# Attention and two mixture-of-experts layers on one core: a front that loads k and v first, gate words a slice earlier, and own buffers for the last sums

## The chip, the cores and the metric

The kernel runs on one core of one Trainium2 chip. The metric is the device time of one execution in microseconds (us); less is better. The engines are TensorE (PE), VectorE (DVE), ScalarE (ACT), GpSimd (POOL) and SyncE (SP), which issues most of the DMAs. Each works through its own queue in order.

## The reference, cut to what matters

`q`, `k` and `v` have 4 batches, 8 heads, 576 tokens and 64 columns a head, all float32. The attention has a softmax of q over the columns and of k over the tokens; then come two layers with 8 experts each.

```
q_s = exp(q - max(q, -1)); q_s /= sum(q_s, -1) + 1e-9
k_s = exp(k - max(k, tokens)); k_s /= sum(k_s, tokens) + 1e-9
kv = einsum('bhsd,bhse->bhde', k_s, v)
x = einsum('bhsd,bhde->bhse', q_s, kv) -> (2304, 512)
expert_idx = argmax(x @ w_gate); gate_w = softmax at expert_idx
x = gate_w * (relu(x @ w1[e]) @ w2[e])     # kept tokens only, capacity 576 an expert
out = x + gate_w2 * (relu(x @ w1b[e]) @ w2b[e])   # where x @ w_skip > 0, else x
```

The second layer has a gate and weights of its own. With these inputs nearly all tokens of a batch go to one expert.

## The kernel before, in words

One batch of 576 tokens is one **group** of a layer: tokens are in the free dimension (two halves of 288), the 512 columns in four chunks of 128 partitions. A group has 16 **slices**: eight of 128 hidden columns for w1 and eight half slices for w2. A slice of w1 is 24 matmuls (two halves, four chunks, three products of high and low parts: `xh`, `xl` of x, `wh`, `wl` of the weights). Split into high and low (`split`, L773): ACT casts (L774), DVE subtracts (L775). ACT evacuates a w1 slice with relu (`hh`, L868), DVE takes the rest (`hl`, L869); both are operands of the w2 slices (L855). Two PSUM tiles, `pair`, alternate between slices.

The order of the work is written out by hand. `COURSE` (L44) has five groups, (layer, batch): (0,0), (0,1), (0,2), (1,0), (1,1). For each of the 16 slices it has a line of words, before the bar and behind it; the loop at the end emits `products(i)`, the split of the weights for slice i+2, the words before the bar, `evacuate(i)`, and the words behind it. A word such as `e.km` is a step of half a batch of attention (a, b: first batch; c, d: second; e, f: third; g, i: fourth, of which no full group is made): `qm` maxima of q, `q1` to `q3` exponentials, `qn` normalisation, `km`, `kt`, `kc`, `ke` the maxima of k, their transposition, subtraction and exponential, `kv` the product k v, `qt` transposes of q, `re` the product with kv. `C1.6` is step 6 of the routing of batch 1. `G.1` and `G.2` make the group's gate a row on all partitions: `gate1` (L903) computes the gate words `gm` on DVE (`gate_weights`, L893: hi, gm, gm), transposes them on PE (pgm, L907), and sends them through DRAM; `gate2` reads them back. Since PE's queue is in order, the next slice stands behind that transposition.

Before the first group stands the **front** (L938 to L1045), written as straight code for the halves a and b of batch 0. Loads are issued on SP in the order q, k of a, k, q of b, then v of both; `warm_up(n)` (L529) issues n matmuls on constants that nobody reads. When one token's x is ready (token 512), `guess` (L560) makes its logits (pgu, L565) and names the expert whose weights SP loads for the group, ahead of the routing; steps 5 and 6 of the routing compare the guess with the list of experts found (L724), and a miss counts into `beyond`. If that is positive at the end, a general branch computes all again. C1.g and C2.g make the same guess for batches 1 and 2. `first_products` (L804) then does the first two slices of group (0,0) in one piece; the course goes on behind them with `C0.1` (pl, L586) and c's maxima of k.

At the end, `evacuate` of a last group multiplies with the gate into `yt` and adds it to x (L886 to L888). `yt` has the tag "ot", a ring of three buffers that the output tiles of `Store` have too; an output tile is free when its DMA has landed.

Of the kernel before, what the change touches and what calls it, by code (L numbers as in the profile page):

```python
# [45 lines left out]
    L4 c.qm | C0.1  # L46
    c.km c.q1 | c.kt
# [18 lines left out]
    L5 C1.6 e.q2 | e.kc  # L66
# [17 lines left out]
    L5 S.p M0.3 | S.g0 M0.4  # L84
# [15 lines left out]
    L4 | g.rw  # L100
# [17 lines left out]
    L4 | T.t03 O0.2  # L118
# [20 lines left out]
def kernel(  # L139
# [410 lines left out]
    class Route:  # L550
# [9 lines left out]
        def guess(self):  # L560

            g = GUESS.index(self.s[1])
            pt = bank("pgu")
            for c in range(NC):
                nc.tensor.matmul(  # L565
                    out=pt[0:1, 0:E], lhsT=self.chunk(c, slice(4 * P, 4 * P + 1)), rhs=self.weights[:, c, 0:E],
                    start=(c == 0), stop=(c == NC - 1),
                )
# [208 lines left out]
    class Group:  # L777
# [26 lines left out]
        def first_products(self):  # L804

            pts = [banks() for _ in range(2)]
            for cs in (range(0, 2), range(2, 4)):
                for s in range(2):
                    wh, wl = whs[s % NB], wls[s % NB]
                    for a in range(2):  # L810
                        for c in cs:
                            for n, (u, w) in enumerate(((wh, xh), (wh, xl), (wl, xh))):
                                nc.tensor.matmul(  # L813
                                    out=pts[s][:, a, :HT],
                                    lhsT=u[:, c],
                                    rhs=w[:, c, tokens(a)],
                                    start=(c == 0 and n == 0),
                                    stop=(c == NC - 1 and n == 2),
                                )
            return pts  # L820

        early = ()
# [40 lines left out]
        def evacuate(self, s):  # L863
# [22 lines left out]
            t = halves(hp.tile([P, S], F32, name="yt", tag="ot", bufs=3))[:, w]  # L886
# [16 lines left out]
        def gate1(self):  # L903

            self.gate_weights()
# [33 lines left out]
    with tc.tile_pool(name="fp", bufs=1) as fp:  # L939
        warm16 = fp.tile([P, 3 * P], F16, name="warm16")  # L940
        nc.vector.memset(warm16, 1.0)
        warm_up(34)
        a, b = [Half(0, hh, X[0], fp, 1) for hh in range(2)]
        a.load_q()
        a.load_k()
        b.load_k()
        b.load_q()
        a.load_v()
        b.load_v()
        H["c"].load_q()  # L950
        H["c"].load_k()
        a.room()
        b.room()
        j4 = [(h, 4) for h in range(HH)]
        a.qm()
        a.exps(j4 + [i for i in HJ if i not in j4])
# [4 lines left out]
        a.kc()  # L961
        warm_up(5)
        b.kt_()
        a.ke()
        warm_up(7)
        b.kc_max()
        a.inverse()
        a.norm(j=slice(4, 5))
        b.kc_sub()
        warm_up(2)  # L970
        a.kv1()
        b.ke()
        b.qm()
        a.norm(slice(0, 2), F4)
        pt = bank("ptq")
        a.turn_new()
        a.turn(0, pt)
        a.kv2()
        nc.scalar.copy(a.qT[:, 0, 0:4 * P], pt)
        b.exps(j4)  # L980
        b.exp_sub(slice(0, 2), F4)
        b.kv1()
        b.exps([(2, j) for j in range(4)])
        b.exp_act(slice(0, 2), F4)
        b.inverse(j=slice(4, 5))
        b.norm(j=slice(4, 5))
        a.norm(slice(2, 4), F4)
        p4 = bank("ptq4")
        b.turn_new()
        a.turn_last(p4)  # L990
        b.turn_last(p4, 2 * LAST)
        a.to_last(nc.scalar.copy, a.qT, p4)
        b.to_last(nc.scalar.copy, b.qT, p4, 2 * LAST)
        b.exps([(3, j) for j in range(4)])
        pt = bank("ptq")
        a.turn(1, pt)
        nc.scalar.copy(a.qT[:, 1, 0:4 * P], pt)
        px = bank("px4")
        a.out_last(px)
        b.sum_bulk(slice(0, 2), F4)  # L1000
        b.kv2()
        b.out_last(px, 2 * LAST)
# [8 lines left out]
        first.load(0, 0)  # L1011
        first.load(0, 1)
        first.load(1)
        H["c"].load_v()
        first.load(2)
        H["d"].load_q()
        H["d"].load_k()
# [397 lines left out]
```

## Time and profile before

| what | before |
|---|---|
| median of 3 runs (lowest to highest) | 442.55 us (441.36 to 442.78) |
| the profiled execution, its span | 443.49 us, 441.7 us |
| PE busy, share of the span | 403.4 us, 91% |
| DVE busy, ACT busy | 250.1 us (57%), 185.8 us (42%) |
| mean granted TensorE clock | 0.948 of full speed |

All times below are from the start of the span. Busy time of PE is modelled and its ends overlap; what a slice takes is better read from the chain of waits or from starts that follow each other. In a table of stretches PEclk is the granted clock as a share of full speed (2.4 GHz); 0.50 is the lower level (1.2 GHz). A name behind an arrow in brackets is what ended an idle time.

### The profile page before, as it was taken

Reading aid. Unit: us, or ns where it says so; the run is one execution under the profiler, and the core shown is the slowest. Engines: PE = TensorE matmul, PEld = TensorE weight load, DVE = VectorE, ACT = ScalarE, POOL = GpSimd, SP = SyncE. Lnnn points to the kernel's source line nnn. Section 1 sums busy time; section 2 is a strip of 40 time slices with the busy share of each in tenths; the row PEclk is TensorE's granted clock in tenths of the full one; section 3 lists DMA queues with packets and bytes.
Section 4 is the critical chain, followed back from the end, with each engine's and each line's share of the span. In section 5 each row is a group of like instructions: output and inputs, shape, how many; then the busy total and the mean of one; then the engine's idle time right before and its main releaser. Section 6 shows DMA issues by size and latency. Waiting matters only on the chain.

```text
span 441.7 us, 8583 instructions
## 1 busy us (share of the span) xinstructions
PE 403.4 (91%) x3297; PEld 359.2 (81%) x3297; DVE 250.1 (57%) x636; ACT 185.8 (42%) x570; POOL 8.3 (2%) x34
## 2 busy tenths in 40 slices
PE   8896799999996999999999999888999999899891
PEld 4673698988996989898999888778998988699881
DVE  3955259743686556357636655366576735554431
ACT  4646357563347474324246522322375333231211
POOL 3000000000000000000000000000000000000000
PEclk9958879999998899999999999998999999999996
DMA  8809812600770400095255671116135555273133
GB/s 210 245 1 258 196 47 88 170 1 1 247 201 0 124 1 1 2 310 137 60 206 174 200 221 47 49 49 217 49 96 170 169 171 177 74 213 132 35 101 84
DMA packets 72537, 54.50 MB, mean 123 GB/s; under 512 B 18455, under 2 KB 67115, under 8 KB 72491
## 3 DMA queue, kind: packets, MB, share of 16 engines
q1 hardware_dynamic: 70536, 53.60, 41.6%
q10 hardware_dynamic: 1954, 0.31, 0.5%
q8 instruction: 27, 0.44, 0.4%
q14 instruction: 20, 0.16, 0.1%
HBM read 49.16 MB, written 4.73 MB: 122 GB/s over the span
## 4 chain that ended last, share of the span: by engine, by line
PE 76%; DVE 10%; ACT 7%; issue 3%; DMA 2%; SPq 0%; DVEq 0%; ACTq 0%
PE pair L855 28%; PE pair L834 24%; PE pk L437 4%; PE pair L813 2%; PE px L495 2%; PE ptq L463 2%; PE pl L586 2%; PE pxs L1084 2%; ACT eq L334 2%; ACT hh L868 1%; PE pto L1218 1%; DMA kt<-in_k_dram 1%; PE py L1140 1%; PE ph L1140 1%; DVE wl L775 1%
## 5 line engine op out<-in xcount | busy, mean ns | idle before, releaser
L855 PE MATMUL pair<-hh,wh 128*128 128x288 f32 x320 | 98.0, 306 | 0.0
L834 PE MATMUL pair<-xh,wh 128*128 128x288 f32 x304 | 96.1, 316 | 0.0
L855 PE MATMUL pair<-hl,wh 128*128 128x288 f32 x320 | 94.4, 295 | 0.0
L855 PE MATMUL pair<-hh,wl 128*128 128x288 f32 x320 | 94.2, 294 | 0.0
L834 PE MATMUL pair<-xl,wh 128*128 128x288 f32 x304 | 92.3, 304 | 0.0
L834 PE MATMUL pair<-xh,wl 128*128 128x288 f32 x304 | 92.1, 303 | 0.0
L775 DVE TENSOR_TENSOR wl<-ws,wh 128x512 fp32r<-128x512 f32 x80 | 54.9, 686 | 38.1 <-ACT wh L774 37.1
L868 ACT ACTIVATE hh<-pair 128x576 fp32r<-128x576 f32 x40 | 25.9, 648 | 108.9 <-PE pair L834 100.1
L869 DVE SCALAR_TENSOR_TENSOR hl<-pair,hh 128x576 fp32r<-128x576 f32 x40 | 30.3, 756 | 62.9 <-ACT hh L868 62.9
L855 PEld LDWEIGHTS pair<-hh,wh 128*128 128x128 f32 x320 | 60.2, 188 | 3.8 <-issue 1.6
L834 PEld LDWEIGHTS pair<-xh,wh 128*128 128x128 f32 x304 | 60.0, 197 | 2.2 <-issue 0.9
L855 PEld LDWEIGHTS pair<-hl,wh 128*128 128x128 f32 x320 | 60.2, 188 | 0.1
L834 PEld LDWEIGHTS pair<-xl,wh 128*128 128x128 f32 x304 | 60.1, 198 | 0.1
L855 PEld LDWEIGHTS pair<-hh,wl 128*128 128x128 f32 x320 | 60.1, 188 | 0.0
L834 PEld LDWEIGHTS pair<-xh,wl 128*128 128x128 f32 x304 | 59.8, 197 | 0.0
L334 ACT ACTIVATE eq<-qt,mx 128x64 f32<-128x64 f32 x152 | 50.7, 337 | 4.7 <-DVE mx L323 4.7
L774 ACT CAST wh<-ws 128x512 fp32r<-128x512 f32 x80 | 49.1, 619 | 2.7 <-DMA ws<-in_moe_w_dram 2.1
L334 ACT ACTIVATION_READ_ACCUMULATOR eq<-qt,mx 128x1 f32 x152 | 28.8, 189 | 0.0
L775 DVE TENSOR_TENSOR xl<-x,xh 128x576 fp32r<-128x576 f32 x20 | 15.0, 753 | 9.0 <-ACT xh L774 9.0
L1219 ACT COPY ot<-pto 128x256 f32<-128x256 f32 (+1 forms) x24 | 7.0, 316 | 28.3 <-PE pto L1218 21.2
L411 ACT ACTIVATE kt<-kt 128x1280 f32<-128x1280 f32 x8 | 10.2, 1272 | 13.8 <-issue 7.1
L437 PE MATMUL pk<-vt,kt 128*64 128x64 f32 (+3 forms) x320 | 15.9, 242 | 0.0
(196 smaller groups left out, 499.8 us busy)
## 6 DMA issues: line engine op xcount, KB each, us to landing
ws<-in_moe_w_dram SPq DMA_DIRECT2D x39, 512.0 KB, 4.9
tw<-in_moe_w_dram SPq DMA_DIRECT2D x24, 512.0 KB, 4.4
qt<-in_q_dram SPq DMA_DIRECT2D x8, 512.0 KB, 7.8
kt<-in_k_dram SPq DMA_DIRECT2D x8, 512.0 KB, 7.5
out_dram<-ot SPq DMA_DIRECT2D x12, 256.0 KB, 2.7
vt<-in_v_dram SPq DMA_DIRECT2D x4, 512.0 KB, 7.0
vt<-in_v_dram SPq DMA_DIRECT2D x16, 128.0 KB, 5.4
mg<-gate SPq DMA_DIRECT2D x4, 288.0 KB, 6.0
```

The lines of the kernel that those rows point to most:

```text
L334: nc.scalar.activation(self.eqv[:, h, j], self.qt[:, h, j], AF.Exp, bias=self.mx[:, i:i + 1], accum_out=self.qz[:, i:i + 1])
L411: nc.scalar.activation(self.kt, self.kt, AF.Exp)
L437: nc.tensor.matmul(out=pk[64 * g:64 * g + 64, c * D1 + o:c * D1 + o + n], lhsT=self.kt[:rows(j), 2 * c + g, j], rhs=ones32[:rows(j), 0:1] ...
L463: nc.tensor.transpose(pt[:, j * P:(j + 1) * P], self.eqf[:, j, c * P:(c + 1) * P], ident)
L495: nc.tensor.matmul(out=pt, lhsT=self.kd[:, c], rhs=self.qT[:, c, 0:4 * P], start=True, stop=True)
L586: nc.tensor.matmul(out=pl[32 * c:32 * c + 32, :HT], lhsT=self.weights[:, c], rhs=self.chunk(c, tokens(a)), start=True, stop=True,)
L774: nc.scalar.copy(hi, src)
L775: nc.vector.tensor_tensor(out=lo, in0=src, in1=hi.bitcast(F32), op=ALU.subtract)
L834: nc.tensor.matmul(out=self.pt[:, a, :HT], lhsT=u[:, c], rhs=w[:, c, tokens(a)], start=(c == 0 and n == 0), stop=(c == NC - 1 and n == 2),)
L855: nc.tensor.matmul(out=self.pt[:, a, :HT], lhsT=p_[:, f], rhs=w[:, tokens(a)], start=(v == 0 and f == 0 and n == 0), stop=(v == 1 and f == ...
L868: nc.scalar.activation(halves(hh), src, AF.Relu)
L869: nc.vector.scalar_tensor_tensor(out=halves(hl), in0=src, scalar=0.0, in1=halves(hh).bitcast(F32), op0=ALU.max, op1=ALU.subtract,)
```

## The change

1. The front. SP loads k of a, k of b, v of a, q of a, v of b, q of b; c's k is loaded only after the first group's first weights. The k path of both halves stands first, with kv for both; then the guess; then q of a and of b, in halves of two heads (five blocks of 64 columns each, one half as DVE addition and one ACT exponential, the other as ten small exponentials, where before token block 4 had its own pass). `warm_up` has 24 instead of 34 at the start and other counts between the steps. `set_capacity` (one matmul and two DVE copies) moves from the front's end to behind b's transposes of maxima.
2. The guess has another input: the sums of the rows of kv (four matmuls of kv with a column of ones, pgx, and a DVE copy gx). All three guesses are made so.
3. The first two slices are done in four parts: the first two chunks of either slice, then the last two. The splits of x and of the weights stand between.
4. `gate_weights` is a word of its own, G.3, one to four slices ahead of G.1.
5. In the last group `yt` takes buffers of another tag ("kqv", seven).
6. In the first line of group (0,0) c.km stands behind `C0.1` and not a slice later.

```diff
     ((0, 0), """
-    L4 c.qm | C0.1
-    c.km c.q1 | c.kt
+    L4 c.qm | C0.1 c.km
+    c.q1 | c.kt
...
-    L5 C1.6 e.q2 | e.kc
+    L5 C1.6 e.q2 | G.3 e.kc
...
-    L5 S.p M0.3 | S.g0 M0.4
+    L5 G.3 S.p M0.3 | S.g0 M0.4
...
-    L4 | g.rw
+    L4 G.3 | g.rw
...
-    L4 | T.t03 O0.2
+    L4 G.3 | T.t03 O0.2
...
             g = GUESS.index(self.s[1])
+            pt = bank("pgx")
+            for c in range(NC):
+                nc.tensor.matmul(
+                    out=pt[:, c:c + 1], lhsT=kvd[c // 2][:, c % 2], rhs=ones32[:, 0:1], start=True, stop=True
+                )
+            gx = self.tl([P, NC], "gx")
+            nc.vector.tensor_copy(out=gx, in_=pt[:, 0:NC])
             pt = bank("pgu")
             for c in range(NC):
                 nc.tensor.matmul(
-                    out=pt[0:1, 0:E], lhsT=self.chunk(c, slice(4 * P, 4 * P + 1)), rhs=self.weights[:, c, 0:E],
+                    out=pt[0:1, 0:E], lhsT=gx[:, c:c + 1], rhs=self.weights[:, c, 0:E],
...
-            t = halves(hp.tile([P, S], F32, name="yt", tag="ot", bufs=3))[:, w]
+            if self.last:
+                t = ap.tile([P, S], F32, name="yt", tag="kqv", bufs=7)
+            else:
+                t = hp.tile([P, S], F32, name="yt", tag="ot", bufs=3)
+            t = halves(t)[:, w]
...
         def gate1(self):
 
-            self.gate_weights()
...
+        def first_products(self, s, cs):
+
+            if cs[0] == 0:
+                self.early = self.early + [banks()]
+            wh, wl = whs[s % NB], wls[s % NB]
+            for a in range(2):
+                for c in cs:
+                    for n, (u, w) in enumerate(((wh, xh), (wh, xl), (wl, xh))):
...
-        warm_up(34)
+        warm_up(24)
         a, b = [Half(0, hh, X[0], fp, 1) for hh in range(2)]
-        a.load_q()
         a.load_k()
         b.load_k()
+        a.load_v()
+        a.load_q()
+        b.load_v()
         b.load_q()
-        a.load_v()
-        b.load_v()
         H["c"].load_q()
-        H["c"].load_k()
...
+        a.km()
+        a.kt_()
+        warm_up(4)
+        b.km()
+        a.kc_max()
+        warm_up(5)
+        a.kc_sub()
+        a.ke()
+        b.kt_()
+        warm_up(5)
+        set_capacity()
+        b.kc_max()
+        warm_up(3)
+        b.kc_sub()
+        a.kv1()
+        b.ke()
+        a.qm()
+        a.exps([(2, j) for j in range(NJ)])
+        a.exp_sub(H01, slice(0, NJ))
+        a.exp_act(H01, slice(0, NJ))
+        warm_up(4)
+        b.kv1()
+        a.exps([(3, j) for j in range(NJ)])
+        a.kv2()
+        b.kv2()
+        warm_up(3)
+        a.sum_bulk(H01, slice(0, NJ))
         RT["C0"].guess()
         first.eid = load_reg(gid[0], [ET.SP], 7)
         first.load(0, 0)
         first.load(0, 1)
         first.load(1)
+        H["c"].load_k()
+        first.load(2)
         H["c"].load_v()
-        first.load(2)
         H["d"].load_q()
         H["d"].load_k()
         first.load(3)
         H["d"].load_v()
...
+        q_norm(a, H01)
+        b.qm()
+        b.exp_sub(H01, slice(0, NJ))
+        a.turn_new()
+        warm_up(3)
+        q_turn(a, 0)
+        b.exps([(2, j) for j in range(NJ)])
+        q_norm(a, H23)
+        b.exp_act(H01, slice(0, NJ))
+        warm_up(3)
+        q_turn(a, 1)
+        q_last(a)
+        x_main(a, 0)
+        b.sum_bulk(H01, slice(0, NJ))
+        b.exps([(3, j) for j in range(NJ)])
+        x_main(a, 1)
+        x_last(a)
+        q_norm(b, H01)
+        first.split_x(0)
+        first.split_x(1)
+        first.split_w(0)
+        q_norm(b, H23)
+        b.turn_new()
+        q_turn(b, 0)
+        first.first_products(0, range(0, 2))
+        q_turn(b, 1)
+        q_last(b)
+        x_main(b, 0)
+        first.split_w(1)
+        x_last(b)
+        x_main(b, 1)
+        first.first_products(1, range(0, 2))
+        first.split_x(2)
+        first.split_x(3)
+        first.first_products(0, range(2, 4))
+        first.first_products(1, range(2, 4))
```

**Three places in the order of instructions.** The first is DVE in group (0,1), from the end of routing step 6 (gw) to the copy of the transposed gate words (gT); kt is e's subtraction of maxima, mx f's maxima of q. Before:

```order
L747 RECIPROCAL gw_136<-gw_136 128x5
L869 SCALAR_TENSOR_TENSOR hl<-pair_84,hh 128x576
L404 TENSOR_TENSOR kt<-kt,pmax 128x1280
L775 TENSOR_TENSOR wl_207<-ws_200,wh_203 128x512
L320 TENSOR_REDUCE mx<-qt 128x20
L323 TENSOR_SCALAR mx<-mx 128x20
L869 SCALAR_TENSOR_TENSOR hl<-pair_83,hh 128x576
L897 TENSOR_SCALAR hi<-dlo_137 128x1
L898 SCALAR_TENSOR_TENSOR gm<-z_135,dlo_137,gw_136 128x5
L901 SCALAR_TENSOR_TENSOR gm<-z_135,hi,gm 128x5
L909 COPY gT<-pgm 5x128
```

and now:

```order
L754 RECIPROCAL gw_136<-gw_136 128x5
L874 SCALAR_TENSOR_TENSOR hl<-pair_83,hh 128x576
L906 TENSOR_SCALAR hi<-dlo_137 128x1
L907 SCALAR_TENSOR_TENSOR gm<-z_135,dlo_137,gw_136 128x5
L910 SCALAR_TENSOR_TENSOR gm<-z_135,hi,gm 128x5
L404 TENSOR_TENSOR kt<-kt,pmax 128x1280
L782 TENSOR_TENSOR wl_207<-ws_200,wh_203 128x512
L320 TENSOR_REDUCE mx<-qt 128x20
L323 TENSOR_SCALAR mx<-mx 128x20
L874 SCALAR_TENSOR_TENSOR hl<-pair_84,hh 128x576
L917 COPY gT<-pgm 5x128
```

The three instructions that make gm moved up past kt, a weight split, both mx and one hl. (Behind the change the lines of the code are other ones: L897 is L906 now.)

The second is DVE in the front, from kv of half b to the guess (gid) and beyond. Before:

```order
L458 TENSOR_TENSOR kvd_115<-pk,rz 64x2x64 x2
L362 TENSOR_SCALAR qz<-qz 128x2x4
L363 RECIPROCAL qz<-qz 128x2x4
L1004 COPY x_121<-px_489 128x4x64
L367 TENSOR_TENSOR eq<-eq,qz 128x2x4x64
L571 TENSOR_REDUCE gmx<-pgu 1x1
L572 SCALAR_TENSOR_TENSOR gsc<-pgu,gmx,c_85 1x8
L575 TENSOR_REDUCE gkey_107<-gsc 1x1
L576 TENSOR_SCALAR gid_110<-gkey_107 1x1
L577 TENSOR_SCALAR gid_110<-gid_110 1x1
```

and now:

```order
L458 TENSOR_TENSOR kvd_115<-pk,rz 64x2x64 x2
L348 TENSOR_REDUCE qz<-eq 128x10
L569 COPY gx<-pgx 128x4
L578 TENSOR_REDUCE gmx<-pgu 1x1
L579 SCALAR_TENSOR_TENSOR gsc<-pgu,gmx,c_85 1x8
L582 TENSOR_REDUCE gkey_107<-gsc 1x1
L583 TENSOR_SCALAR gid_110<-gkey_107 1x1
L584 TENSOR_SCALAR gid_110<-gid_110 1x1
L362 TENSOR_SCALAR qz<-qz 128x10
L363 RECIPROCAL qz<-qz 128x10
L367 TENSOR_TENSOR eq<-eq,qz 128x2x5x64
L320 TENSOR_REDUCE mx<-qt 128x20
```

The copy of x (L1004) that fed the guess is gone; the copy gx of the sums and q's row sums (qz) stand ahead of it, and b's maxima of q (mx) and its subtraction follow the guess instead of preceding kv.

The third is DVE at the program's end, with the semaphores that an instruction waits for (DMAHW are those of the DMA queues); ot is an output tile. Before:

```order
L1219 COPY ot<-pto 128x256 [waits DMAHW1_49,DMAHW2_49,PE_49,Activation_49]
L1219 COPY ot<-pto 128x256 [waits DVE_49,PE_49]
L1219 COPY ot<-pto 128x256 [waits DMAHW3_49,DMAHW4_49,PE_49,Activation_49]
L887 TENSOR_TENSOR yt<-pair_83,mg 128x288 [waits DMAHW0_49,DMAHW7_49,DVE_49,Activation_49]
L888 TENSOR_TENSOR x_122<-x_122,yt 128x288 [waits DVE_49]
L1219 COPY ot<-pto 128x256 [waits DMAHW6_49,DMAHW5_49,PE_49]
```

and now:

```order
L1234 COPY ot<-pto 128x256 [waits DMAHW7_49,DMAHW0_49,PE_49]
L1234 COPY ot<-pto 128x256 [waits DMAHW1_49,DMAHW2_49,PE_49,Activation_49]
L1234 COPY ot<-pto 128x256 [waits DMAHW3_49,DMAHW4_49,PE_49,Activation_49]
L896 TENSOR_TENSOR yt<-pair_84,mg 128x288
L897 TENSOR_TENSOR x_122<-x_122,yt 128x288 [waits DVE_49]
L1234 COPY ot<-pto 128x256 [waits DMAHW5_49,DMAHW6_49,PE_49,Activation_49]
```

The order is the same; the last yt no longer waits for a DMA semaphore.

## Rows read from the trace of the kernel before

**Rows 1.** The page, busy time: us, share of the span, instructions.

```profile
PE 403.4 (91%) x3297; PEld 359.2 (81%) x3297; DVE 250.1 (57%) x636; ACT 185.8 (42%) x570; POOL 8.3 (2%) x34
```

**Rows 2.** What PE waited for, whole span: us in total, times, longest.

```profile
PE pgm L907 <- DVE gm L901: 7.9, 4, 4.1
PE pt L386 <- DVE m L380: 4.5, 3, 3.4
...
PE pto L1218 <- DVE x L888: 3.0, 1, 3.0
```

**Rows 3.** Stretches, PE: length, busy (instructions), clock, DMA share, GB/s.

```profile
20.49:34.14 13.65, 13.65 (x117) 0.50 0.06 18
...
137.10:141.19 4.09, 0.00 (x0) 0.85 0.00 0
141.19:147.07 5.88, 5.88 (x25) 0.52 0.55 137
294.98:296.97 1.99, 0.00 (x1) 1.00 0.00 0
296.97:300.38 3.41, 3.41 (x15) 0.50 0.24 72
```

**Rows 4.** Chain that ended last, 130 to 160: start, length, what.

```profile
136.24 1.48 DVE kt L404
...
140.82 0.24 DVE gm L901
...
147.14 1.76 PE pk L437 x40
148.90 6.55 PE pair L834 x48
...
156.96 3.05 PE pair L834 x23
```

**Rows 5.** Timeline of PE at two pgm: start, length, instruction, idle before.

```profile
215.92 0.27 PE L907 MATMUL pgm<-c,gm 128*5 128x128 f32 x1 [0.80 <-DVE gm L901]
...
380.52 0.27 PE L907 MATMUL pgm<-c,gm 128*5 128x128 f32 x1 [0.99 <-DVE gm L901]
```

**Rows 6.** Chain that ended last, 36 to 62.

```profile
41.94 9.21 PE pair L813 x48
...
55.68 0.66 PE pt L386 x2
56.34 5.55 PE pair L834 x24
```

**Rows 7.** Timeline of the front, DVE, PE and SP.

```profile
6.17 1.49 DVE L320 TENSOR_REDUCE mx<-qt 128x20 f32<-128x1280 f32 x1 [4.67 <-DMA qt<-in_q_dram]
...
8.56 0.69 DVE L378 TENSOR_TENSOR m<-kt 128x512 f32<-128x512 f32 x1 [0.69 <-DMA kt<-in_k_dram]
...
24.95 1.32 PE L437 MATMUL pk<-ones,kt 128*64 128x1 f32 x20
...
32.18 1.54 SPq L792 DMA_DIRECT2D ws<-in_moe_w_dram  x3
```

**Rows 8.** Groups of instructions, 0 to 62: busy us, mean ns, idle before.

```profile
L334 ACT ACTIVATE eq<-qt,mx 128x64 f32<-128x64 f32 x46 | 15.3, 336 | 4.7 <-DVE mx L323 4.7
...
L320 DVE TENSOR_REDUCE mx<-qt 128x20 f32<-128x1280 f32 x3 | 4.4, 1481 | 4.7 <-DMA qt<-in_q_dram 4.7
...
L367 DVE TENSOR_TENSOR eq<-eq,qz 128x512 f32<-128x512 f32 (+1 forms) x6 | 3.5, 599 | 0.1
```

**Rows 9.** Timeline of PE at the second guess.

```profile
109.17 0.55 PE L489 MATMUL px<-qT,kvd 128*128 128x64 f32 x4
...
110.18 0.24 PE L565 MATMUL pgu<-wg,x 128*1 128x8 f32 x4 [0.28 <-ACT x L475]
```

**Rows 10.** Timeline of DVE at the end.

```profile
431.42 0.42 DVE L1219 COPY ot<-pto 128x256 f32<-128x256 f32 x1 [0.53 <-PE pto L1218]
433.98 0.46 DVE L887 TENSOR_TENSOR yt<-pair,mg 128x288 f32<-128x288 f32 x1 [2.13 <-DMA out_dram<-ot]
```

More of the change, by code (lines that the diff above doesn't have):

```diff
@@ L802, in split_x @@
             split(xh[:, c], xl[:, c], (self.x if src is None else src)[:, c])
[L804 to L822, printed above, removed]
+        def first_products(self, s, cs):
[5 more added lines that the diff above has]
+                    for n, (u, w) in enumerate(((wh, xh), (wh, xl), (wl, xh))):
+                        nc.tensor.matmul(
+                            out=self.early[s][:, a, :HT],
+                            lhsT=u[:, c],
+                            rhs=w[:, c, tokens(a)],
+                            start=(c == 0 and n == 0),
+                            stop=(c == NC - 1 and n == 2),
+                        )
+        early = []
         def products(self, s):
@@ L941 @@
         nc.vector.memset(warm16, 1.0)
-        warm_up(34)
+        warm_up(24)
         a, b = [Half(0, hh, X[0], fp, 1) for hh in range(2)]
-        a.load_q()
         a.load_k()
         b.load_k()
+        a.load_v()
+        a.load_q()
+        b.load_v()
         b.load_q()
-        a.load_v()
-        b.load_v()
         H["c"].load_q()
-        H["c"].load_k()
         a.room()
         b.room()
-        j4 = [(h, 4) for h in range(HH)]
-        a.qm()
-        a.exps(j4 + [i for i in HJ if i not in j4])
+        H01, H23 = slice(0, 2), slice(2, 4)
         a.km()
@@ L1019, with q_norm @@
         H["d"].load_v()
-        b.inverse(slice(2, 4), F4)
-        b.norm(slice(2, 4), F4)
-        def x_out(h, c):
-            o = 2 * h.hh + c
-            pt = bank("px")
-            h.out_main(c, pt)
-            nc.scalar.copy(X[0][:, o, 0:4 * P], pt)
-            return lambda: first.split_x(o)
+        def q_norm(h, hs):
+            h.inverse(hs)
+            h.norm(hs)
         def q_turn(h, c):
@@ L1033, in q_turn, with q_last, x_main, x_last @@
             nc.scalar.copy(h.qT[:, c, 0:4 * P], pt)
-        sp = [x_out(a, 0)]
+        def q_last(h):
+            pt = bank("ptq4")
+            h.turn_last(pt)
+            h.to_last(nc.scalar.copy, h.qT, pt)
+        def x_main(h, c):
+            pt = bank("px")
+            h.out_main(c, pt)
+            nc.scalar.copy(X[0][:, 2 * h.hh + c, 0:4 * P], pt)
+        def x_last(h):
+            pt = bank("px4")
+            h.out_last(pt)
+            h.to_last(nc.vector.tensor_copy, X[0][:, 2 * h.hh:2 * h.hh + 2], pt)
+        q_norm(a, H01)
[21 more added lines that the diff above has]
+        b.turn_new()
         q_turn(b, 0)
-        sp.append(x_out(a, 1))
-        sp.pop(0)()
-        sp.pop(0)()
+        first.first_products(0, range(0, 2))
         q_turn(b, 1)
-        x_out(b, 0)()
-        first.split_w(0)
-        x_out(b, 1)()
+        q_last(b)
+        x_main(b, 0)
         first.split_w(1)
-        set_capacity()
-        first.early = first.first_products()
+        x_last(b)
[5 more added lines that the diff above has]
+        first.first_products(1, range(2, 4))
     hp = ctx.enter_context(tc.tile_pool(name="hp", bufs=1, reuse_waits="tile"))
@@ L1263, in word @@
         elif name == "G":
-            (groups[k].gate, groups[k].gate1, groups[k].gate2)[int(rest)]()
+            (groups[k].gate, groups[k].gate1, groups[k].gate2, groups[k].gate_weights)[int(rest)]()
         elif name[0] == "L":
```

40 lines of the change are left out of this document (removed).

## The prediction

> **What bounds the kernel now.** I read the page's busy times first. TensorE (PE) is busy for 91% of the span [rows 1], so a change can win only where PE waits, or where its clock is low. The second view is the list of what PE waits for [rows 2]. Three waits stand at its head: PE waits four times, 7.9 us together, for the gate word gm, for 4.5 us in the transposes of k's maxima, and for 3.0 us in the last stores. The third view is the table of stretches with the granted clock [rows 3]. Read it for what a pause costs beyond itself: after the pause from 137.10 to 141.19 the next slice ran at 0.52 of full speed, and after the pause from 294.98 to 296.97 the clock was at its lower level (1.2 GHz) for 3.41 us. The front has such a stretch from 20.49 to 34.14, and the pace shows another: the 24 matmuls of the third dense slice took 5.55 us, 0.23 each [rows 6], while at full clock a slice takes 3.2 to 3.3, as 48 matmuls take 6.55 in the chain [rows 4].
>
> **Gate words.** The order shows hi and both gm instructions ahead of e.kc's subtraction; before, they stand behind it, one weight split, f's q maxima and an hl. In the chain that leads to the first of the four waits [rows 4] the subtraction begins at 136.24 and the last gm at 140.82; between them f's maxima alone take 1.48 [rows 8]. With the three gm instructions (0.5 us) first, gm is ready at 136.8, and PE, done with its slice at 137.1, goes on. What is late next? I follow the queues by the same rows. The next slice runs 137.4 to 140.6 and e's pk (1.76) to 142.4; the slice after it needs the hl that now ends at 141.1, half a microsecond later than in the old order, and is not held. Two slices more end at 148.8, the transposes of q take 1.2, and there VectorE (DVE) is late: f's maxima end at about 150.4. The slice behind them starts at 150.85, where it started at 156.96 [rows 4]: **6.1 us**. No more than 4.1 of pause and 2.6 of clock (5.88 less 3.2 and the transposition) can come back; if DVE only moves the pause, perhaps 3.
>
> The other three [rows 3, 5]: 0.8 us at 215.92; 1.99 at 296.97; 0.99 at 380.52. At none is another input late: the weight splits of the next slice are done before the pause begins. At the second of these the clock adds to it: the 15 instructions in 3.41 us [rows 3] are some 14 matmuls, which at 0.133 take 1.9, so 1.5 more. By the rows the drop follows the pause of 1.99 us. The Trainium skill's page "TensorE: Matmul & The Clock Gate", section "Why this matters for your kernels", lets only longer idle gaps than this one cost the clock; by it the sum would be 1.5 smaller. I go by the row. Gate words together: 6.1 + 0.8 + 3.5 + 0.9 = **11.3 us**, bounds 7 and 12.
>
> **Last sums.** In the last group yt has its own tag, and the order shows that its wait on the DMA queues is gone. The yt at 433.98 waited 2.13 us for an output DMA; DVE's copy before it ended at 431.84 [rows 10], and PE was not what it waited for. It starts at 431.9: **2.1 us**, bounds 1.5 and 2.5. What follows (the addition, five transposes, copies, the last DMA) is unchanged and moves up whole.
>
> **Guess for the second and third batch.** This costs. PE spends 0.70 us there now: the two rows for pgu with the wait of 0.28 between them [rows 9], 109.66 to 110.36. The change puts four matmuls with kvd as weights ahead, a copy on DVE that PE waits for, and pgu again. A float32 matmul is recorded as two passes, so eight: at most 0.137 each, as for the same weights with 64 columns (0.55 for four [rows 9]), at least 0.04, by the passes of pk with one column at twice the half-clock rate (1.32 for 20 [rows 7]). The weights are those of the first row, so I take 0.9, with 0.28 for the copy and its two hand-overs and 0.25 for pgu: 1.45, so 0.75 more. DVE is idle around it. Twice: **-1.5 us**, bounds -0.5 and -2.
>
> **Front.** The first load lands at 6.17, where DVE waited for q; k came at 8.56 [rows 7]. Now k has that place: 2.4 earlier. It loses 0.3 of this behind the 24 warm-ups, which end at 8.2, and about a microsecond because the capacity matmul (0.55, and DVE's copy behind it) now stands ahead of b's broadcast of maxima. SyncE's loads move with k; its queue order k, k, v, q, v, q brings v and q before they are asked for. So a's pk starts at 15.35; b's starts at 19.5 and, at half clock from 20.5, ends at 24.4 instead of 26.27 [rows 7]. The guess follows: kvd 1.0, eight passes at half clock 1.4, copy 0.2, pgu 0.35, five small DVE instructions 1.0, to 28.5; registers and issue take 0.7, so the weights are asked for at 29.2, where it was 32.18 [rows 7]. They are not late afterwards; neither is c's k, behind them on SyncE.
>
> Now q is late. DVE's rows give 1.48 for a half's maxima and 0.6 on average for a normalisation of 256 or 512 columns, by which I put 0.86 for the 640 that it now has [rows 8]; ScalarE (ACT) takes 0.33 for each of the remaining 20 exponentials [rows 8]. Down both queues from 28.5: a normalised, b's maxima and subtraction, a's second half to 33.3; ACT's exponentials and copies to 37.8; x and the first weights split at 40.5. The first quarter of the dense slices then starts at 40.5 to 41.2, where the dense work began at 41.94 [rows 6]. But each later quarter waits for its own copies. ACT casts the last part of x by 49.2, DVE has its rest at 50.1, and 24 matmuls (3.2) later both slices end at **53.3**, 2.2 us *later* than now (51.15 [rows 6]). It is given back behind it. Now PE does the gate products and stands until 55.68, because c's maxima come after a weight split that itself waits for ACT [rows 6]; in the change c.km stands ahead of that split, ends at 54.8, and the third slice starts at 55.5 instead of 56.34: 0.9. And since PE no longer pauses there, I expect this slice at full clock: 2.4 more. **3.3 us**, bounds -1 (half clock from 17 on and in the third slice) and 8 (full clock throughout). I take the lower half since the order of work that had the half clock, pk and transposes, is still there.
>
> **Sum.** 11.3 + 2.1 - 1.5 + 3.3 = 15.2. The profiled execution took 443.49 us, of which 441.7 are its span: 428.3 for one like it. It lay 0.94 above the median of the runs, 442.55, from which I take 15.2: **427.4 us**. Moving the terms inside their nearer bounds gives this case 425 to 430.
>
> **Rivals.**
> *The clock stays low in the front.* For it: fewer warm-ups, and the clock was at half for 13.65 us with PE busy throughout [rows 3]. Against: the slices of early products follow each other closely. The front then gives nothing: 430.7. Chance 0.15.
> *The clock stays high in the front.* The warm-ups between the small matmuls could hold it. The front gives 8: 422.7. Chance 0.12.
> *The gate's wait gives place to another.* PE would wait for hl, a split or f's maxima behind it, since DVE has little room from 136 to 141. The first gives 3 and the third only its pause, 6.7 in place of 11.3, less another microsecond of follow-on waits: 433. Chance 0.10.
> *The half clock behind the two pauses has another cause* and stays: 2.6 + 1.5 less, 431.5. Both low stretches begin within a pause or at its end [rows 3], so only 0.06. The rule of the Trainium skill named above would keep the 1.5 of these.
> *Slower: the guess names another expert.* It decides at the comparison of the guess with the routed list: one miss in three batches makes "beyond" positive, and the general branch computes everything again. Five groups take some 386 us from 56 on, so eight more cost over 600 us: above 1,000. By the formula on the reference's inputs, the old and the new guess both give experts 0, 3 and 6, the ones to which most tokens of those batches go. Chance 0.02.
> The forecast keeps 0.55.
>
> **Numbers.** About 0.3%, 1.3 us, is what a measurement of this kernel can tell from no change. All cases but the last end far below; I leave 0.02 for terms that cancel each other. Faster 0.96, same 0.02, slower 0.02. The range takes in the forecast's own bounds, both cases of the front and the two losses of the clock and the gate: 422.5 to 433.
>
> **What would show it.** Right: PE's wait for gm gone from the list of waits, no low clock behind the slices near 135 and 285; yt without a DMA wait; the first weight DMA near 29; the third slice starting near 55 at full clock. Wrong: a new wait of PE of over 2 us on hl, wl or a copy; the first weight DMA after 31; PE at half clock past 48; a span above 435.

## The result and the profile after

The changed kernel takes 430.99 us (median of four runs, 429.69 to 432.30) against 442.02 for the kernel before, measured beside it on the same chip (441.36 to 442.78): a ratio of 0.975, with a 95% interval from 0.971 to 0.979, or 11.0 us less. 427.4 was forecast, within 422.5 to 433. The direction is right and the time lies in the range, but 3.6 above the forecast. The profiled execution took 431.83 us with a span of 429.9; the one before had 441.7, so between the two traces 11.8 us are to be found, where my sum has 15.2.

First the page's busy time and row of the clock, after the change:

```profile
PE 399.4 (93%) x3321; PEld 353.7 (82%) x3321; DVE 252.5 (59%) x640; ACT 182.3 (42%) x547; POOL 8.4 (2%) x34
PEclk9956898999999999999999999999999999999997
```

PE has the work that it had before [rows 1], and the 24 passes of pgx for the three new guesses, in a shorter span. Next what PE waited for over the whole span (us in total, times, longest):

```profile
PE ptq L463 <- DVE eq L367: 3.6, 2, 2.4
PE pts L1204 <- DVE x L1208: 2.7, 3, 1.2
PE pp L644 <- DVE oh L636: 2.2, 2, 1.1
PE pp L644 <- DVE oh L632: 2.1, 1, 2.1
PE pt L386 <- DVE m L380: 1.7, 3, 0.6
...
PE pmax L398 <- DVE dm L392: 1.3, 2, 0.9
...
PE pto L1233 <- DVE x L897: 0.8, 1, 0.8
```

The 7.9 us for gm that headed the list before [rows 2] are gone, the 4.5 for k's maxima are 1.7, and the 3.0 of the last stores are 0.8. The wait for a tile `oh` at L632, the choice of experts for the first batch, has grown from 0.9 to 2.1 (it stood at L625 before); the two waits for `oh` at L636, 1.1 each, belong to two later routings. New are the waits at the head of the list, 1.2 and 2.4 for `eq`, the normalised q of half a: they lie in the front, at 25.4 and 28.7.

Read one thing in each trace to see where the time went: when PE ends each slice of 24 matmuls. The table has the steps by which that time moved from one slice to the next, before against after, and the forecast's term beside it.

| Place | Before | After | Gain | Forecast |
|---|---|---|---|---|
| first two slices end | 51.14 | 53.18 | -2.04 | -2.2 |
| third slice | 55.99 to 61.87 | 54.96 to 58.38 | 3.49 in all | 3.3 in all |
| fourth slice | 62.50 to 66.03 | 60.18 to 63.70 | 2.33 in all | as above |
| fifth slice | 67.67 to 71.11 | 66.64 to 71.38 | **-0.27 in all** | **3.3 in all** |
| guesses near 110 and 180 | | | -0.76, -0.75 | -0.75, -0.75 |
| first gate place, with the next four slices | 141.22 to 147.14 | 138.00 to 141.42 | 6.75 - 0.79 = 5.96 | 6.1 |
| second | 215.94 | 211.28 | 0.97 - 0.47 = 0.50 | 0.8 |
| third | 297.00 to 301.96 | 290.17 to 293.59 | 3.69 | 3.5 |
| fourth | 380.55 | 371.16 | 1.04 | 0.9 |
| end of the last slice to the end of the span | 11.7 | 9.3 | 2.4 | 2.1 |

The steps add up to 11.8. Every term but one came out within 0.3 of the forecast. The one is the front, and even there the forecast is right up to the third slice. Then 3.8 us are lost in two slices, 1.16 ahead of the fourth and 2.60 at the fifth. Ahead of the fourth, PE waits 0.9 for `dm` (L398 in the list of waits), which DVE makes behind an hl that waits for ACT. This is the table of stretches in the front, at these places and at two gates (length, busy and instructions of PE, PEld, DVE, ACT and POOL, granted clock, DMA share, GB/s):

```profile
21.76:35.41 13.65, 9.77 (x38) 5.92 (x37) 8.61 (x20) 4.45 (x17) 0.99 (x2) 0.50 0.61 163
38.83:45.65 6.82, 6.51 (x20) 4.84 (x21) 2.23 (x5) 1.37 (x4) 0.00 (x0) 0.50 1.10 297
54.96:58.38 3.42, 3.42 (x28) 3.42 (x28) 0.91 (x2) 3.42 (x17) 0.00 (x0) 1.00 0.33 96
63.70:65.84 2.14, 0.00 (x0) 0.00 (x1) 2.00 (x8) 1.62 (x2) 0.00 (x0) 1.00 0.00 1
66.13:69.55 3.42, 3.42 (x24) 3.35 (x21) 3.28 (x12) 2.41 (x13) 0.00 (x0) 0.50 0.45 136
137.90:141.42 3.52, 3.52 (x29) 3.31 (x29) 3.49 (x5) 2.10 (x3) 0.00 (x0) 1.00 0.00 0
290.17:293.59 3.42, 3.42 (x29) 3.42 (x27) 2.73 (x11) 1.40 (x3) 0.00 (x0) 1.00 0.00 1
```

The third slice and the slices behind both gates run at full clock. Before, the two behind the gates had 3.41 us or more at the lower level [rows 3], and the third slice took 5.55 [rows 6]. But from 63.70 to 65.84 PE does nothing while DVE is busy for 2.00 of 2.14, and behind that pause the clock is at its lower level for 3.42, so that the fifth slice takes 4.74 where it took 3.44. The chain of waits through that place shows what PE waited for (start, length, what):

```profile
59.64 1.32 ACT eq L334 x8
60.96 0.55 ACT hh L873
...
61.53 0.76 DVE hl L874
62.29 0.33 DVE L L608
62.62 0.12 DVE L L614
62.74 1.39 DVE kt L404
64.14 0.60 DVE wl L782
64.74 0.12 DVE mx L625
...
65.58 0.21 DVE oh L632
65.80 0.05 issue
65.84 0.26 PE pp L644 x4
...
66.71 4.68 PE pair L839 x24
```

PE ended the third slice at 58.38, but ACT copies it (hh) only at 60.9, behind c's exponentials of q. VectorE (DVE) then has hl, the sums of the routing's scores (L608), c's subtraction (kt) and a weight split (wl) ahead of the five small instructions that end in oh. The same places in the kernel before, ACT's copy first, then PE's first row behind oh (idle before in brackets):

```profile
61.91 0.65 ACT L868 ACTIVATE hh<-pair 128x576 fp32r<-128x576 f32 x1 [2.98 <-PE pair L834]
66.90 0.26 PE L637 MATMUL pp<-oh,c 128*128 128x32 f16 x4 [0.88 <-DVE oh L625]
```

There ACT stood 2.98 us waiting for the half-clock slice. After the change PE is early and ACT and DVE are not: hh comes 1.04 earlier, PE 3.5. Of those 2.98 ACT itself could give no more than about one: its exponentials of q begin 2.03 later than before (55.16 for 53.13), as the first two slices end 2.04 later.

### The profile page after: what moved, and what is told of

Read it like the earlier page. It is cut to its first block, busy times and chain, and to the rows that moved or that the text cites. A ratio compares the mean times of both kernels' runs of the same rounds, so it can differ in the third digit from the quotient of the medians.

```text
span 429.9 us, 8608 instructions
## 1 busy us (share of the span) xinstructions
PE 399.4 (93%) x3321; PEld 353.7 (82%) x3321; DVE 252.5 (59%) x640; ACT 182.3 (42%) x547; POOL 8.4 (2%) x34
## 4 chain that ended last, share of the span: by engine, by line
PE 72%; DVE 7%; ACT 4%; issue 1%; ACTq 0%; DVEq 0%
PE pair L860 29%; PE pair L839 23%; PE pk L437 2%; PE pxs L1099 2%; PE pl L593 2%; PE pto L1233 1%; PE py L1155 1%; PE ph L1155 1%; PE pts L1204 1%; ACT hh L873 1%; PE px L495 1%; DVE wl L782 1%; ACT eq L334 1%; PE ptq L463 1%; DVE hl L874 1%
## 5 line engine op out<-in xcount | busy, mean ns | idle before, releaser
L839 PE MATMUL pair<-xh,wh 128*128 128x288 f32 x304 | 93.5, 308 | 0.0
L839 PE MATMUL pair<-xl,wh 128*128 128x288 f32 x304 | 90.1, 296 | 0.0
L839 PE MATMUL pair<-xh,wl 128*128 128x288 f32 x304 | 89.9, 296 | 0.0
L839 PEld LDWEIGHTS pair<-xh,wh 128*128 128x128 f32 x304 | 57.6, 190 | 2.3 <-issue 0.9
L839 PEld LDWEIGHTS pair<-xl,wh 128*128 128x128 f32 x304 | 57.7, 190 | 0.1
L839 PEld LDWEIGHTS pair<-xh,wl 128*128 128x128 f32 x304 | 57.6, 190 | 0.0
L334 ACT ACTIVATE eq<-qt,mx 128x64 f32<-128x64 f32 x140 | 46.8, 339 | 0.3 <-DVE mx L323 0.3
L334 ACT ACTIVATION_READ_ACCUMULATOR eq<-qt,mx 128x1 f32 x140 | 26.7, 190 | 0.0
L463 PE MATMUL ptq<-c,eq 128*128 128x128 f32 x64 | 10.4, 307 | 5.6 <-DVE eq L367 3.6
```

What stands on the lines that cost most here:

```text
L334: nc.scalar.activation(self.eqv[:, h, j], self.qt[:, h, j], AF.Exp, bias=self.mx[:, i:i + 1], accum_out=self.qz[:, i:i + 1])
L463: nc.tensor.transpose(pt[:, j * P:(j + 1) * P], self.eqf[:, j, c * P:(c + 1) * P], ident)
L839: nc.tensor.matmul(out=self.pt[:, a, :HT], lhsT=u[:, c], rhs=w[:, c, tokens(a)], start=(c == 0 and n == 0), stop=(c == NC - 1 and n == 2),)
```

## The experiments

**Theory A**: the words, sums and guesses are worth what the table says; the front's gain is real up to the third slice and is held up behind it, because there ACT and DVE hold the work and the first batch's routing comes late. **Rivals**: B, the parts depend on each other, and the front's gain went elsewhere; C, the clock falls for other causes than PE's pauses; D, whatever is moved out of the way, the next thing in the queue takes its place. E (PE's half clock and not DVE holds the front) and F (the new front is worth nothing) come up with their runs.

### The front alone, and the words and sums alone

The second run is the kernel before with only the words and sums, of which the lines below are the main ones (and `gate1` without its call of `gate_weights`, which becomes the word G.3). The first is the changed kernel with the same lines taken back and the later guesses as before, so that the new front is all it has:

```diff
-    L5 C1.6 e.q2 | e.kc
+    L5 C1.6 e.q2 | G.3 e.kc
...
-    L5 S.p M0.3 | S.g0 M0.4
+    L5 G.3 S.p M0.3 | S.g0 M0.4
...
-    L4 | g.rw
+    L4 G.3 | g.rw
...
-    L4 | T.t03 O0.2
+    L4 G.3 | T.t03 O0.2
...
-            t = halves(hp.tile([P, S], F32, name="yt", tag="ot", bufs=3))[:, w]
+            if self.last:
+                t = ap.tile([P, S], F32, name="yt", tag="kqv", bufs=7)
...
```

> The front alone: gate words, last sums and the guess for the second and third batch are as in the kernel before. Theory A (the front's gain is real up to the third slice and is given back in the two slices behind it, where the routing of the first batch is late): third slice over at 58.4 instead of 61.9, fifth slice over at 71.4 as in the changed kernel and 0.3 later than the 71.1 of the kernel before, from there on no difference: the time is that of the kernel before, 442.0, plus 0.3 (441.5 to 443). Rival B (the front gives its 3.3 through to the end, and something else in the changed kernel ate it): 438.7, fifth slice over at 67.8.

> The kernel before with the gate words a slice ahead and the last sums in their own buffers, and nothing else. Theory A: the steps of the two traces add up, 6.0 + 0.5 + 3.7 + 1.05 at the four gate places and 2.4 at the end, 13.6 together: 428.4 from 442.0, which is 2.6 below the changed kernel. Rival B (front and words depend on each other, and the words gain less without the new front): 430 to 433. PE's wait for gm is gone from the list of waits and there is no half clock behind 137 and 285 in either case.

The front alone: 441.17 (ten runs) against 441.34 (thirteen), ratio 0.9996 [0.9965, 1.0027]: no change. Its third slice ends at 58.37 and its fifth at 71.39, just as A said. The words and sums alone: 429.73, ratio 0.9745 [0.9693, 0.9797]. A said 428.4; the trace gives 6.0, 0.5, 3.7 and 1.0 at the four places again. By these steps B falls, though the median alone, at the edge of B's 430 to 433, would not have settled it: the words don't need the new front, and everything that the change brought is in them and in the last sums. The changed kernel is not faster than this run; its front gives nothing and its two later guesses cost.

The median is 1.3 above A's number. The likely reason is to be seen in the runs of the kernel before: they spread from 439.06 to 443.49 and follow the granted clock of the run, 0.948 in those from 443.25 on, 0.963 or 0.967 in those at 439.1. Its profiled execution had 0.948. So part of what I took from that trace as clock is not lost in every run. The trace of the front alone shows it, in the stretches of the first and the third gate place, where its old waits for gm still stand:

```profile
137.39:141.48 4.09, 0.00 (x0) 0.00 (x0) 3.91 (x8) 3.33 (x10) 0.00 (x0) 0.97 0.00 0
141.25:144.66 3.41, 3.14 (x14) 3.17 (x15) 1.00 (x3) 1.21 (x8) 0.00 (x0) 0.50 0.10 29
294.22:296.21 1.99, 0.01 (x1) 0.00 (x0) 1.34 (x6) 1.16 (x2) 0.00 (x0) 1.00 0.00 0
296.25:299.67 3.42, 3.42 (x27) 3.42 (x28) 1.96 (x9) 0.24 (x1) 0.00 (x0) 1.00 0.27 80
```

At the third gate the pause is 1.99 as in rows 3, and the slice behind it keeps full clock. At the first the pause of 4.1 is followed by 3.41 at half clock, where the kernel before had 6.83 (139.96 to 146.78): its slice takes 4.84 instead of 5.92.

### The routing's word a line earlier

```diff
-    L5 c.q2 | C0.2 c.kc
-    C0.3 c.ke d.qm | C0.4
+    L5 c.q2 | C0.2 C0.3 c.kc
+    c.ke d.qm | C0.4
```

> The changed kernel with the third word of the first batch's routing (five small DVE instructions up to oh) one line earlier, ahead of c's subtraction and of a weight split. Theory A: oh is there at 63.9 instead of 65.8, PE's wait for it falls from 2.1 to under 0.3, and with the wait the half clock in the fifth slice goes (3.45 instead of 4.75): 3.2 less, 427.8 against 431.0. Rival C (the clock falls there whatever PE waited for): the wait alone, 1.9 less, 429.1. Rival D (what now stands behind the routing, c's subtraction and the split, makes PE wait in its place): 430 to 431, with a new wait on pk or wl between 64 and 72.

In the trace the wait for oh is 0.3, the fifth slice takes 3.45, and from the end of the third slice PE has gained 3.20 on the changed kernel by then: A's number, not C's 1.9, in this execution. But at the eighth slice 1.27 of it is lost again, to d's maxima of k. This is the chain of waits to that place; between the rows left out it stays on DVE:

```profile
61.89 0.76 DVE hl L874
...
64.18 1.48 DVE kt L404
65.66 0.60 DVE wl L782
66.26 1.41 DVE mx L320
...
77.50 0.61 DVE m L378
78.13 0.44 DVE m L379
...
78.65 0.43 DVE m L380
79.08 0.14 issue
79.22 0.41 PE pt L386 x2
```

DVE has hardly a gap in 17 us. So D holds in part: moving one word leaves DVE's queue as long as it was, and the block begins when hh comes. The runs, 430.64 (428.57 to 433.37), ratio 0.9777 [0.9706, 0.9849], miss A's 427.8, lie in D's 430 to 431 and can't be told from the changed kernel.

### PE kept at work in a gate's pause

```diff
             pt = bank("pgm")
+            if self.m == 1 and not self.last:
+                for _ in range(12):
+                    nc.tensor.matmul(out=pt[:, :3 * P], lhsT=tri16, rhs=c16, start=True, stop=True)
             nc.tensor.transpose(pt[0:NJ, 0:P], self.gm, ident)
```

> The kernel before, with 12 filler matmuls of 384 float16 columns ahead of the transposition of gm in the gate words of the fourth group (the place of the 1.99 us wait at 294.98), so that PE works while it waits for gm; their result is overwritten. Theory A (the clock fell because PE stood still): the pause is as long as before or up to 0.2 longer, but the slice behind it runs at full clock, 3.45 instead of 4.96: 1.3 to 1.5 less than the kernel before. Rival C (the clock falls there for another cause, or PE must stand still for longer): the slice takes 4.96 as before, time unchanged or 0.2 longer.

A single run, 442.25, shows no gain; the table of stretches tells more:

```profile
293.79:295.93 2.14, 2.13 (x14) 1.09 (x12) 1.49 (x6) 1.16 (x2) 0.00 (x0) 1.00 0.00 0
295.96:299.39 3.43, 3.43 (x27) 3.43 (x28) 1.96 (x9) 0.24 (x1) 0.00 (x0) 1.00 0.33 101
303.55:304.69 1.14, 0.01 (x1) 0.01 (x1) 1.00 (x7) 1.14 (x3) 0.00 (x0) 1.00 1.03 413
306.19:309.60 3.41, 3.41 (x17) 3.41 (x16) 1.87 (x14) 0.00 (x0) 0.00 (x0) 0.50 0.15 38
```

The filled pause is followed by full clock: 1.54 gained there. But two slices on a pause of 1.14, which in the kernel before cost nothing beyond itself, is followed, 1.50 after its end, by 3.41 at half clock, and 1.53 is lost. As the front alone kept full clock behind an unfilled pause, the first half of this proves little by itself.

### c's exponentials behind the copies

```diff
-    c.q1 | c.kt
-    L5 c.q2 | C0.2 c.kc
-    C0.3 c.ke d.qm | C0.4
+    | c.q1 c.kt
+    L5 | c.q2 C0.2 C0.3 c.kc
+    c.ke d.qm | C0.4
```

> The changed kernel with the routing's third word a line earlier (as in the run before) and c's exponentials of q behind the first copies hh of their lines on ACT, instead of ahead of them. The run with the routing alone showed VectorE without a gap from 61.9 to 79, so theory A now reads: what holds PE from the third to the eighth slice is VectorE's queue, which begins when hh comes. Expected: hh of the third slice at 58.8 instead of 60.9, oh at 61.6, no wait of PE over 0.5 for dm or oh, fourth slice over at 62.9, and VectorE's block of work over some 2.2 earlier than with the routing alone, so that the eighth slice starts at 77.0 to 77.6 instead of 80.96: 3.4 to 4 less than the changed kernel, 427.3. Rival D (VectorE isn't what holds PE there, but transfers or ACT's exponentials, which are as many as before): the eighth slice starts no earlier than with the routing alone, 79.0 to 79.4: 429.

427.68, ratio 0.9665 [0.9612, 0.9718], against the forecast 427.3. ACT's copy of the third slice, which ended at 59.68 in this trace, and what follows on DVE:

```profile
59.84 0.65 ACT L873 ACTIVATE hh<-pair 128x576 fp32r<-128x576 f32 x1
62.76 0.20 DVE L632 TENSOR_TENSOR oh<-sc,fm 128x40 f16<-128x40 f32 x1
77.30 0.43 DVE L380 TENSOR_TENSOR m<-m,kt 128x256 f32<-128x256 f32 x1
```

From the end of the third slice to the start of the eighth is 22.58 in the changed kernel, 20.65 with the routing's word earlier, and 18.36 here (78.04 less 59.68): 4.2 come back, where 3.4 to 4 were expected. It was 18.82 before the change. The front of this execution was itself 1.30 later at the third slice, and the gain in the trace 3.2. At this place A holds against D.

### The front: its clock, its order, the old guess

Three runs. The first fills three of PE's pauses in the changed kernel's front; the second has the exponentials behind and moves a's sums; the third also gives the second and third batch the old guess.

```diff
         a.turn_new()
-        warm_up(3)
+        warm_up(7)
         q_turn(a, 0)
...
-        warm_up(3)
+        warm_up(10)
         q_turn(a, 1)
...
         b.turn_new()
+        warm_up(5)
         q_turn(b, 0)
```

> The changed kernel with 16 more filler matmuls in three pauses of PE in the front (4 at 25.4, 7 at 28.7, 5 at 36.3; at half clock 0.33 each, so that they fill the pauses of 1.24, 2.38 and 1.67 and no more). Theory A (the half clock of the front follows PE's pauses): the low stretch that ends at 35.41 ends one stretch earlier, the second one, from 38.83 on, goes in part, and as PE is what holds the work from 32.5 to 47 (ACT and VectorE wait for it there), both first slices end 1.5 to 4 earlier than 53.18. Of this the same is left behind the fifth slice, since everything behind starts from there: 427 to 429.5. Rival C (the clock is low there for the kind of work, small products and transposes, not for the pauses): the low stretches stay, 53.2 plus or minus 0.3, 431.

426.65 (425.40 to 430.19), ratio 0.967 [0.960, 0.974]. Of the front's low stretches, 13.65 and 6.82 us in the table above, one of 6.82 is left:

```profile
22.70:29.52 6.82, 6.55 (x30) 3.87 (x31) 5.72 (x16) 1.79 (x9) 0.00 (x0) 0.50 0.34 89
29.52:48.28 18.76, 16.32 (x94) 11.31 (x96) 11.26 (x21) 11.57 (x32) 0.99 (x2) 1.00 1.02 263
```

Both first slices end at 48.28, 4.90 earlier, more than the 1.5 to 4 expected, and all of it comes through (6.28 at the last slice, with the 1.33 of a fifth slice at full clock). PE still waits 2.1 for oh, but the queues ahead of oh begin as much earlier as PE does, and that pause was not followed by half clock here. The interval overlaps the changed kernel's, so the size rests on the trace; one of the four runs, the one at 430.19, had a clock of 0.974 where the others had 0.986.

```diff
         a.kv2()
+        a.sum_bulk(H01, slice(0, NJ))
+        a.inverse(H01)
+        a.norm(H01)
         b.kv2()
         warm_up(3)
-        a.sum_bulk(H01, slice(0, NJ))
...
-        q_norm(a, H01)
         b.qm()
```

> As the run with c's exponentials behind, and in the front a's sums and its first normalisation stand ahead of b's kvd on VectorE, which waits 3.0 for b's pk at 18.5 to 21.5 with that work behind it. Theory A: VectorE's queue holds the front too. a's normalisation ends at 21.2 instead of 26.4, b's maxima begin at 25.3 instead of 26.4, all behind them and both first slices end 1.1 earlier (52.1), and 1.1 comes through to the end: 426.2 if the run with the exponentials behind gives 427.3, in any case 0.8 to 1.3 less than it. Rival E (PE at half clock holds the front, not VectorE): the first slices end at 53.2 as before, no difference between these two runs.

427.45, ratio 0.9643 [0.9584, 0.9703]: not to be told from 427.68. In its trace the front is 0.77 ahead of the run it builds on although the clock was low from 17.92 to 45.23, so neither A nor E is shown; the front's clock differs from one execution to the next by more than this edit is worth.

```diff
+            gx = None
+            if g == 0:
...
+                u = self.chunk(c, slice(4 * P, 4 * P + 1)) if gx is None else gx[:, c:c + 1]
```

> As the run with the front's sums ahead, and the guess for the second and third batch as in the kernel before (its last token's row, no sums of k v), the first batch's as in the change. The traces showed 0.76 and 0.75 for the two new guesses. Theory A: 1.5 less than the run with the front's sums ahead, 424.7; PE stands 0.70 at each of the two places instead of 1.46.

424.78, ratio 0.9615 [0.9543, 0.9687]. The steps at the two guesses are 0.74 and 0.73, as expected. The traces differ by more in stretches of half clock: the front is 2.25 ahead here, and a slice in the fourth group 1.53 behind, so the 2.7 between the medians is not all the guesses'.

### The old front under the same words, and all together

The next run is the kernel before with the two diffs of the words and sums and of c's exponentials: it differs from the run with the old guess too in the front alone. The last takes that run, with the new front, fills two of the front's pauses (9 and 6 more matmuls, as in the diff above) and moves two more routing words:

```diff
-    C2.6 | M0.2
-    L5 G.3 S.p M0.3 | S.g0 M0.4
+    C2.6 | M0.2 M0.3
+    L5 G.3 S.p | S.g0 M0.4
...
-    M2.6 | M1.2
-    L7 T.p M1.3 T.l G.2 | T.g0 M1.4
+    M2.6 | M1.2 M1.3
+    L7 T.p T.l G.2 | T.g0 M1.4
```

> The run with the old guess too, but with the front of the kernel before in place of the new one: so both have the gate words, the last sums, the earlier routing word and c's exponentials behind, and differ in the front alone. Theory A (the new front's gain is real up to the third slice and was held up by the routing and VectorE's queue behind it; with these moved it comes through): the old front's third slice ends 2.5 to 4 later, and so does the run: 427 to 429 against 424.8. Rival F (the new front is worth nothing, whatever stands behind it): 424 to 425.5.

> As the run with the old guess too, with filler matmuls in the front's two pauses (9 more ahead of the turn of a's second half, 6 ahead of b's) and the third routing word of two later routings (the ones whose oh PE waited 1.1 for, twice) a line earlier each. Theory A: the waits for oh go, 2.2 less; in the front the half clock ends earlier and both first slices end near 46 to 48 instead of 51.5, of which all comes through: 4 less. Together 418.5, between 417 and 421. If the words only hand the wait on (rival D), 2.2 more than that; if the fillers don't hold the clock (rival C), 4 more.

The old front: 428.06, ratio 0.9690 [0.9659, 0.9721], by medians 3.3 above the same kernel with the new front (0.9615 [0.9543, 0.9687]; the intervals overlap at their ends). In the traces the new front's third slice ends 5.08 earlier (56.67 for 61.75), and 4.89 of it is still there at the eighth, where in the changed kernel 3.49 had become -0.27 at the fifth. Part of the 5.08 is the clock of one execution; but in the run with a's sums moved, whose front stood at half clock for 27.3, as long as the old front in its trace, the lead is 2.83 at the third slice, and 2.67 of it is left at the eighth. So F falls by the traces: what the front gains comes through once the routing and the exponentials are out of its way.

All together: **418.57** (417.39 to 420.39), ratio 0.9495 [0.9465, 0.9525], 5.05% below the kernel before, its interval clear of the changed kernel's. The page's busy row for PE, and the head of what PE waited for:

```profile
PE 393.9 (95%) x3320; PEld 349.4 (84%) x3320; DVE 251.2 (60%) x638; ACT 182.4 (44%) x547; POOL 8.4 (2%) x34
PE pts L1209 <- DVE x L1213: 2.7, 3, 1.2
PE pt L386 <- DVE m L380: 2.1, 4, 0.6
PE pair L532 <- DVE warm L952: 1.6, 1, 1.6
```

No wait for oh stands in that list any more. The first slices end at 47.55, 3.92 before those of the run that it builds on, and at the two words' places 1.29 and 2.83 are gained, the latter with the 1.5 of a half clock that the earlier run had there. The granted clock of its six runs is 0.978 to 0.989, that of the four without fillers 0.965 to 0.975: so the higher clock doesn't rest on one execution. Fillers and words were not parted here; the run with fillers alone had 0.986 in three of its four, against 0.966 and 0.974 in the changed kernel's.

## Why the prediction was right, and where it failed

**Gate words**: right. 11.2 measured in the trace, 11.3 forecast, with the first place at 5.96 for 6.1. The follow-on wait that I named, f's maxima, is there: the slice behind them starts at 151.78. Up to this gate the changed kernel is 1.03 behind (138.11 for 137.08, by the front and a guess), so on the forecast's clock this is 150.75, where 150.85 was forecast. At the second place 0.47 went back because the gm instructions now stand ahead of a routing word: PE's wait for that oh grew from 0.66 to 1.1, which I had not followed. **Last sums**: right, 2.4 for 2.1; yt starts 1.81 behind the last slice instead of 3.99. **Guess**: right, 1.5. These rows are PE's at the second guess:

```profile
109.85 1.00 PE L565 MATMUL pgx<-ones,kvd 128*128 128x1 f32 x8
111.11 0.34 PE L572 MATMUL pgu<-wg,gx 128*1 128x8 f32 x8 [0.26 <-DVE gx L569]
```

Eight passes take 1.00, where I took 0.9. The lower bound that I gave was wrong: 1.32 for 20 at half clock gives 0.033 each at twice the rate, not 0.04.

**Front**: the term that failed, 3.3 forecast, -0.27 measured; with it nearly all of the 3.4 between 15.2 and 11.8. The steps inside were good where I followed queues: slices over at 53.18 (53.3), ACT's last cast of x over at 49.31 (49.2), c.km over at 54.65 (54.8), the third slice at 54.96 (55.5) and at full clock. They were too careful ahead of that: b's pk ran at full clock until 21.46 (24.4 forecast, at half), so the first weights were asked for at 26.04, 3.2 earlier than I said. It bought nothing: the slices that use them waited for x, which PE made at half clock, as the run with filled pauses shows by its 4.90.

The step that failed is the last one: "2.4 more" at the third slice went into the sum as **3.3 us** of the whole kernel, as if nothing stood behind that slice. The 2.2 were given back and the third slice did run at full clock, 3.49 ahead. But I let the count end there and took it that PE's lead stays; I asked "What is late next?" at the gates and not here. The runs show that the next slices wait for ACT's copy and DVE's queue up to oh, which leaves 1.03 of the lead, and that the half clock behind the wait for oh takes 1.30. Much of the answer was in the trace of before: ACT waited 2.98 for that slice, of which the 2.2 of delay that I had forecast leaves less than one, and PE waited 0.88 for oh. So the lead was worth a microsecond and no more. "Wrong: a new wait of PE of over 2 us" is what came, on tiles other than I named (oh, and eq in the front), and "PE at half clock past 48" came with it, from 66.13 to 69.55.

That the time still lay in the range is luck on this term: -0.27 is within the bounds of -1 and 8, but -1 stood there for a front and a third slice at half clock, and not for a lead that is lost behind it.

**Clock**: I took the drops behind 137.10 and 294.98 as the pauses' doing [rows 3]. At the first gate this is borne out: in the three traces in which its pause of 4.1 stands, the clock falls within it (from 139.96 before, 141.25 in the front alone, 138.93 in the run with PE at work at another gate), and in none of the nine traces with gm ready ahead does a low stretch stand at a gate. What I had not seen is that the drop behind a shorter pause is not certain: the same pause of 1.99 was followed by half clock in one execution and by full clock in another. So the 1.5 is what one execution lost. The Trainium skill's page "TensorE: Matmul & The Clock Gate", section "Why this matters for your kernels", lets only longer idle gaps than the one of 1.99 cost the clock. Here 3.41 at half clock came right behind pauses of 1.99 and 2.14, and 1.4 to 1.5 after pauses of 1.1 in three traces (at 306.19 above, 292.85 with the old guess, 204.57 with the old front), so the measurement decides against the rule as it stands there.

**The rivals**: the time came out near that of "the clock stays low in the front" (430.7), but that rival gave the front nothing because of the clock. Here the third slice had full clock and stood 3.49 ahead with half clock in the front until 45.65, so it was not that; what the front's half clock costs is another matter, 4.90 by the run with filled pauses. That the gate's wait gives place to another happened to the front's slices instead.

## What to carry to other kernels

When an engine is made faster, follow the chain for two more waits than seems needed: read at the next places how long the other engines waited for it before, since that was all the lead that PE could keep here. A lead that ends at another engine's queue is recovered by order, not by speed: here five small instructions and fourteen exponentials, moved by a line or less, gave back 4 us. And take a clock loss from several executions, not from one trace.

## What was not expected of the hardware

The clock's behaviour behind the same pause differs from trace to trace: a pause of 1.99 with and without a drop, pauses of 1.1 and of 2.1 with and without. The thirteen runs of the kernel before that were measured beside the first experiments differ by 4.4 us and follow their granted clock (0.948 to 0.967). In the front the clock could fall with PE at work: in two traces it was low from 17.92 and from 18.11 on, behind small products of k and v that began at 14, with PE at work without a pause since 12.6. Whether these products let it fall was not tried.
